# One matmul loop of a fused attention and MLP kernel: 64-column stationary blocks split into 32-column ones, in the first chunk only

## The chip, the cores and the metric

The kernel runs on one core of a Trainium2 chip. The metric is the device time of one execution in microseconds (us); the median of several runs is compared. Five engines work side by side on a core, each through its own list of instructions: TensorE (PE, the matrix multiplier; its loads of stationary operands are listed apart as PEld), VectorE (DVE), ScalarE (ACT), GpSimd (POOL) and SyncE (SP, which here issues nearly all DMAs). An instruction waits for others through semaphores.

In a matmul one operand, the stationary one, is loaded into TensorE's 128 by 128 array; the other, the moving one, streams through. The contraction runs over the partitions (rows), and the columns of the stationary operand become the partitions of the output in PSUM. If the stationary operand has fewer rows or columns, the array can be cut into tiles: a form such as 128*64 in the profile means 128 rows by 64 columns, so that two such tiles lie side by side in the array. Which of them is used follows from the output's partitions.

## The reference, cut to what matters

Inputs are fp32: q, k, v and alpha of (B=4, H=8, S=768, D=48), and an MLP from 384 to 1536 and back.

```python
for t in range(S):
    state = alpha[:, :, t, :, None] * state + np.einsum('bhd,bhe->bhde', k[:, :, t], v[:, :, t])
    y[:, :, t] = np.einsum('bhd,bhde->bhe', q[:, :, t], state)
...
x = y.transpose(0, 2, 1, 3).reshape(B, S, H * D)
xn = (x - mu) / np.sqrt(var + 1e-06) * g_ln
out = x + np.maximum(xn @ w_ch1, 0.0) @ w_ch2
```

The recurrence is computed in chunks. Within a chunk, y is the masked matrix of scores (q scaled by the running product of alpha, k by its inverse) times v, plus q times the state that the chunk began with.

## The kernel before, in words

The sequence is cut into six chunks of 128 positions, and the work into 24 blocks (chunk c, batch b). One block's attention is the generator `attention(c, b)`. The eight heads are counted as `i` (0 or 1) and `p` (0 to NP - 1 = 3). HS = 64 is half a chunk, and `halves[s]` the partitions of half `s`.

A block goes through: Ln of alpha on ScalarE (L342); its running sum by a triangular matmul (L347 in chunk 0, L354 later); two Exp on ScalarE (L357, L358); k and q scaled on VectorE (L360, L362); both turned by TensorE (L414) and copied out as kT and qT (L418); scores on TensorE (L427 in chunk 0, L442 later); masked copies into the tile `at` on VectorE (L451 in chunk 0, L456 later); the state's update on TensorE (L471), on VectorE and, after chunk 0, GpSimd; then y on TensorE, copied with its sum by ScalarE (L519), the layer norm, and the turned x for the MLP (L565, L567).

Chunk 0 (`whole` in the code) differs: there is no earlier state, so y is the product of `at` and v alone, over all 128 positions at once. The tile `at` is (128, NP, 2, 2, 64): key positions on partitions, then p, i, the half s of the queries, and 64 queries. L497 takes a stationary block of 128 by 64, streams the 48 columns of one head's v through it, and writes 64 partitions of the bank `yps0`. So a block of chunk 0 has 4 x 2 x 2 = 16 such matmuls, and there are four blocks. Chunks 1 to 5 use the other branch (L507), with half-chunks of 64 rows.

The order in which the generators advance is written out by hand in the string `ORDER`, one letter for one step: a to x are the 24 attention blocks (a to d are chunk 0), Y, Z, P, Q chunk 0's MLP, M, V and others the later MLPs, A to H the rounding of the weights. Every engine executes its instructions in the order that results. All of chunk 0's y is one step of each block.

## Time and profile before

| | |
|---|---|
| median of 3 runs | 419.16 us (416.6 to 420.09) |
| the profiled execution, own time | 417.81 us |
| its span, first to last instruction | 416.0 us |
| granted TensorE clock | 1.00 |
| the costliest two lines, matmuls of the MLP in chunks 1 to 5 | L892 32% and L714 31% of the chain that ended last |
| L497, the changed line | 1% of that chain |
| bytes moved by DMA | 61.26 MB, mean 147 GB/s |

How to read it: the span is one execution recorded by the profiler. Busy time of an engine counts the time in which at least one of its instructions was running; matmuls are pipelined, so that neighbouring ones overlap and a busy TensorE is not one at its peak. An fp32 matmul leaves two load records and two matmul records; a transpose by TensorE leaves one of each. The timeline merges neighbouring instructions of a kind into one row with the start of the first, the length up to the end of the last, and their count; the brackets behind it hold the idle time of the engine just before and what ended it. "issue" is time in which the engine waited for nothing that the profile shows.

### The profile page before, as it was taken

To read this page: it belongs to the slowest core of one execution; us is meant where nothing else is said; L and a number is where in the kernel's file an instruction comes from. 1 tells how busy PE (TensorE), PEld (TensorE's weight loads), DVE (VectorE), ACT (ScalarE), POOL (GpSimd) and SP (SyncE) were. 2 spreads that over 40 slices of the span, in tenths; PEclk is the share of its full clock that TensorE was granted. 3 is DMA by queue.
4 is the path that set the end of the run, shared out by engine and by line. 5 is a ranking of instruction groups with operands and counts; after the bars stand their busy time and mean duration, and the time that the engine had idled before them with its cause. 6 is when DMAs were issued, how large, how long until landed. Compare 5 with 4: busy or idle time off the path is not lost.

```text
span 416.0 us, 11451 instructions
## 1 busy us (share of the span) xinstructions
PE 409.0 (98%) x4616; PEld 354.9 (85%) x4616; DVE 292.8 (70%) x554; ACT 217.0 (52%) x522; POOL 122.0 (29%) x134
## 2 busy tenths in 40 slices
PE   7999999999999999999999999999999999999997
PEld 5877888876568889998889998899998889999996
DVE  3897989999997888687268973579533288125754
ACT  4787568774364576245584335773353643245110
POOL 1011013132011562144480254260236321525300
PEclk9999999999999999999999999999999999999999
DMA  8998968888878676945776868536324200000301
GB/s 263 282 272 270 283 141 282 243 169 246 230 139 229 164 151 129 237 100 140 168 144 153 200 167 213 108 45 129 109 58 120 71 1 2 19 0 25 110 20 58
DMA packets 134445, 61.26 MB, mean 147 GB/s; under 512 B 90956, under 2 KB 131276, under 8 KB 134392
## 3 DMA queue, kind: packets, MB, share of 16 engines
q1 hardware_dynamic: 133848, 60.37, 57.5%
q8 instruction: 36, 0.59, 0.6%
q10 hardware_dynamic: 544, 0.17, 0.2%
q14 instruction: 17, 0.14, 0.1%
HBM read 43.12 MB, written 17.39 MB: 145 GB/s over the span
## 4 chain that ended last, share of the span: by engine, by line
PE 94%; ACT 3%; DMA 1%; DVE 0%; issue 0%; SPq 0%; DVEq 0%
PE hps L892 32%; PE ops L714 31%; PE hps L590 8%; PE ops L602 8%; PE yps L507 5%; PE aps L442 3%; PE ups L471 2%; PE tps L414 2%; PE lps L354 2%; DMA ra<-in_alpha_dram 1%; PE aps L427 1%; PE yps L497 1%; PE xps L565 1%; ACT hT L931 0%; ACT lps L358 0%; ACT qT L418 0%
## 5 line engine op out<-in xcount | busy, mean ns | idle before, releaser
L892 PE MATMUL hps<-sum,w 128*128 128x256 f32 x192 | 46.3, 383 | 0.0
L714 PE MATMUL ops<-w,hT 128*128 128x192 f32 x224 | 40.8, 326 | 0.8 <-ACT hT L931 0.8
L892 PEld LDWEIGHTS hps<-sum,w 128*128 128x128 f32 x192 | 35.7, 190 | 6.3 <-ACT u L904 1.7
L738 ACT COPY u<-ops 128x192 f32<-128x192 f32 x30 | 9.5, 316 | 56.4 <-PE ops L714 56.3
L714 PEld LDWEIGHTS ops<-w,hT 128*128 128x128 f32 x224 | 37.2, 190 | 1.4 <-ACT hT L931 1.1
L734 POOL TENSOR_TENSOR ob<-ob,u 128x192 f32<-128x192 f32 x32 | 20.8, 659 | 56.7 <-ACT u L738 33.2
L486 POOL TENSOR_TENSOR mid<-mid,gate 112x192 f32<-112x192 f32 x20 | 14.0, 701 | 77.9 <-DVE mid L484 21.2
L590 PE MATMUL hps<-xT,w 128*128 128x256 f32 x144 | 33.9, 385 | 0.2 <-ACT few L538 0.2
L904 ACT COPY u<-hps 128x512 f32<-128x512 f32 x32 | 18.7, 585 | 28.0 <-PE hps L892 22.1
L892 PE MATMUL hps<-xT,w 128*128 128x256 f32 x136 | 33.3, 379 | 0.0
L602 PE MATMUL ops<-w,hT 128*128 128x384 f32 x96 | 32.6, 491 | 0.0
L590 PEld LDWEIGHTS hps<-xT,w 128*128 128x128 f32 x144 | 26.2, 190 | 4.2 <-ACT few L538 0.4
L904 ACT COPY hT<-hps 128x512 f32<-128x512 f32 x40 | 23.3, 585 | 12.3 <-PE hps L892 12.1
L892 PEld LDWEIGHTS hps<-xT,w 128*128 128x128 f32 x136 | 25.8, 190 | 3.4
L714 PE MATMUL ops<-ws,sum 128*128 128x192 f32 x160 | 28.6, 327 | 0.0
L602 PEld LDWEIGHTS ops<-w,hT 128*128 128x128 f32 x96 | 17.7, 190 | 11.7 <-issue 0.6
L714 PEld LDWEIGHTS ops<-ws,sum 128*128 128x128 f32 x160 | 26.4, 190 | 0.6 <-ACT few L538 0.6
L728 DVE TENSOR_TENSOR ob<-ops,ob 128x192 f32<-128x192 f32 x40 | 13.1, 350 | 16.9 <-POOL ob L734 9.5
L931 ACT ACTIVATE hT<-hT 128x512 f32<-128x512 f32 x40 | 22.9, 621 | 2.1 <-DVE hT L911 2.1
L714 PE MATMUL ops<-ws,hT 128*128 128x192 f32 x128 | 23.4, 326 | 0.0
L714 PE MATMUL ops<-more,sum 128*128 128x192 f32 x120 | 22.2, 328 | 0.0
L731 DVE TENSOR_TENSOR ob<-ob,ops 128x192 f32<-128x192 f32 x35 | 11.8, 349 | 14.0 <-PE ops L714 13.5
(223 smaller groups left out, 1037.9 us busy)
## 6 DMA issues: line engine op xcount, KB each, us to landing
ws<-in_moe_w_ch_dram SPq DMA_DIRECT2D x8, 1152.0 KB
vn<-in_v_dram SPq DMA_DIRECT2D x12, 384.0 KB
kept<-x SPq DMA_DIRECT2D x24, 192.0 KB
ob<-kept SPq DMA_DIRECT2D x24, 192.0 KB
rows<-rj SPq DMA_DIRECT2D x48, 96.0 KB
out_dram<-ob SPq DMA_DIRECT2D x18, 192.0 KB
xrows<-xt SPq DMA_DIRECT2D x64, 48.0 KB
xT<-xrows SPq DMA_DIRECT2D x16, 192.0 KB
```

The source lines that it names most:

```text
L442: nc.tensor.matmul(pair[o][halves[i if o else 1 - i], p, s], k_of[rs, p, s], q_of[rs, p, s], start=True, stop=True)
L486: nc.gpsimd.tensor_mul(new, new, by)
L507: nc.tensor.matmul(yps[j][halves[s], i, p], of, by, skip_group_check=True, start=not (cross and k), stop=k == 1 or not cross)
L590: nc.tensor.matmul(hps, w1[:, f, j * P:(j + 1) * P], xT_of[0][:, f, bs], start=(f == 0), stop=(f == NF - 1))
L602: nc.tensor.matmul(ops_of[b], hT_of[c][:, j, b], w2[:, j], start=(j == 0), stop=(j == NJ - 1))
L714: nc.tensor.matmul(acc, lhs[:, j], rhs[:, j], start=j == 0 and n not in FOLLOWS, stop=j == NT - 1 and n not in FOLLOWS.values(), skip_grou ...
L728: nc.vector.tensor_add(x, acc, x)
L731: nc.vector.tensor_sub(x, x, acc)
L734: getattr(nc.vector if c + 1 == NCB else nc.gpsimd, f"tensor_{op}")(x, x, y)
L892: nc.tensor.matmul(acc[:, i], w, b, start=n not in JOINS and i == 0, stop=n not in JOINS.values(), skip_group_check=True)
L904: nc.scalar.copy(out=copied[n], in_=acc)
L931: nc.scalar.activation(out=x, in_=x, func=AFT.Relu)
```

## The change: 32 queries to a stationary block

In the `whole` branch, the 64 queries of a half are taken in two parts of 32 (`quarters`), each with a matmul of its own: stationary 128 by 32, the same 48 moving columns, 32 output partitions of the same bank. The four parts of the 128 queries lie on four column tiles of 32. The branch for chunks 1 to 5 is untouched.

```diff
         yps = [ps.tile([P, 2, NP, D], FP32, name=f"yps{r}", tag="bank", bufs=6)
                for r in range(1 if whole else 2)]
+        quarters = [slice(u, u + HS // 2) for u in (0, HS // 2)]
+
+        def part(s, o):
+            return slice(HS * s + o.start, HS * s + o.stop)
+
         for p in range(NP):
             if whole:
                 for i in range(2):
                     for s in range(2):
-                        nc.tensor.matmul(yps[0][halves[s], i, p], at[:, p, i, s], vn[:, i, p],
-                                         start=True, stop=True)
+                        for o in quarters:
+                            nc.tensor.matmul(yps[0][part(s, o), i, p], at[:, p, i, s, o],
+                                             vn[:, i, p], start=True, stop=True)
                 continue
```

## The prediction

> **What bounds the kernel now.** I read the page first: the busy shares and the chain of waits.

> ```profile
> PE 409.0 (98%) x4616; PEld 354.9 (85%) x4616; DVE 292.8 (70%) x554; ACT 217.0 (52%) x522; POOL 122.0 (29%) x134
> ...
> PE 94%; ACT 3%; DMA 1%; DVE 0%; issue 0%; SPq 0%; DVEq 0%
> ```

> TensorE is busy for 98% of the span and makes up 94% of the chain; the granted clock is full in all 40 slices. TensorE time saved anywhere is therefore worth its face value unless another engine holds up the same stage. The changed line is L497, so next I asked for that line alone, then for the windows by stage.

> ```profile
> L497 PEld LDWEIGHTS yps<-vn,at x128: 133/138/139, 15.7 to 30.3; 128*64 128x64 f32 x128
> L497 PE MATMUL yps<-vn,at x128: 221/222/258, 15.7 to 30.4; 128*64 128x48 f32 x128
> ...
>   POOL at L525: 7.5, 1
>   ACT x L519: 0.8, 2
> ```

> ```profile
> 15.00:20.00 5.00, 5.00 (x95) 3.76 (x94) 3.86 (x8) 4.16 (x11) 0.00 (x0) 1.00 0.92 247
> 20.00:24.00 4.00, 4.00 (x96) 3.94 (x91) 4.00 (x9) 3.14 (x11) 0.95 (x1) 1.00 1.05 322
> 24.00:28.00 4.00, 3.61 (x101) 2.65 (x101) 3.93 (x7) 3.51 (x11) 0.00 (x0) 1.00 0.93 282
> 28.00:33.00 5.00, 4.80 (x65) 2.87 (x60) 4.08 (x8) 4.97 (x13) 0.95 (x1) 1.00 0.86 216
> 33.00:60.00 27.00, 26.97 (x412) 22.46 (x414) 23.93 (x40) 17.33 (x45) 3.50 (x5) 1.00 0.85 239
> ```

> The line runs only between 15.7 and 30.5 us, while chunk 0's attention is built up. The loop has 4 p by 2 i by 2 s = 16 matmuls in a block and four blocks: 64, and the line shows 128 records, two for each fp32 matmul. In the windows (columns: length, then busy us and count of PE, PEld, DVE, ACT, POOL, clock, DMA) VectorE is full from 20 to 24 us, ScalarE from 28 to 33, and TensorE has holes of 0.39 and 0.20 us. From 33 us TensorE has next to none, so what reaches that point reaches the end.

> The size is read from the timeline: start, length, engine, line, form, count, and in brackets the idle time before.

> ```profile
> 15.69 1.01 PEld L497 LDWEIGHTS yps<-vn,at 128*64 128x64 f32 x32 [0.17 <-issue]
> 15.69 1.14 PE L497 MATMUL yps<-vn,at 128*64 128x48 f32 x32
> 17.57 0.44 PEld L471 LDWEIGHTS ups<-vn,qk 128*48 128x48 f32 x16 [0.60 <-issue]
> 18.06 0.97 PEld L427 LDWEIGHTS aps<-qT,kT 48*128 48x128 f32 x16
> 25.97 1.02 PEld L442 LDWEIGHTS aps<-qT,kT 48*64 48x64 f32 x64
> 36.85 0.45 PEld L471 LDWEIGHTS ups<-vn,qk 64*48 64x48 f32 x32 [0.33 <-issue]
> ```

> **What a group of tiles costs.** 128*64 means 128 rows by 64 stationary columns. L497's s alternates between two column tiles, so its 32 loads are 16 pairs. The merged row ends one load (138 ns) after the last start: (1.01 - 0.138)/15 = 58 ns a pair. L442 has four tiles of 64 columns, 64 loads in 16 fours: (1.02 - 0.135)/15 = 59 ns a four. L471 with 48 columns takes (0.44 - 0.125)/7 = 45 ns a pair at 17.57 and (0.45 - 0.122)/7 = 47 a four at 36.85. L427 with 128 columns: (0.97 - 0.188)/7 = 112 a pair. So a round costs by its columns, not by its number of tiles: about 5 ns plus 0.84 ns a column.

> **What the change does to it.** Each of the 16 matmuls of a block becomes two, with 32 stationary columns each and the same 48 moving columns. That adds 64 matmuls, 128 load records and 128 matmul records over four blocks; multiplications and rounds stay as they are, 16 rounds a block, now of four records on four tiles instead of two on two. No DMA, wait, buffer or other engine's instruction is added, removed or moved. The PSUM bank and the next reader, L519 on ScalarE, are the same.

> Price of a new round: by the columns of its load alone 5 + 0.84 x 32 = 32 ns; but 48 moving columns must also pass. L471, with 48 stationary and 48 moving, gives 45, and cannot tell which 48 sets it; L354, with 384 moving on 64 stationary, shows that the moving side can set the pace (0.88 us for two rounds). The upper end from these rows is L497's own 58, at which splitting brings nothing. I take 45, the only rows with 48 moving that are not held by 64 loaded columns. A block then takes 16 x 45 = 0.72 us instead of 16 x 58 = 0.93: 0.21 us less. Four blocks: 0.84 us, between 0 (at 58) and 16 x 26 x 4 = 1.66 us (at 32).

> [...]

> **How much of it reaches 33 us.** Block 0, 15.69: L354 follows at 16.76 on TensorE, and its last input, the ScalarE Ln, ended at 16.37, so 0.2 us goes through; VectorE's masked copy at 19.25 had waited 0.97 us on TensorE's scores and moves by the same. Blocks 1 and 2, 20.13 to 22.17: ScalarE's copy of y at 22.21 waited 0.35 for them, and its copies of kT and qT follow, on which TensorE's scores at 24.88 wait 0.39. Here up to 0.6 us can pass. But VectorE works from 19.25 to 29.7 nearly without a gap and only had the first 0.2; block 3 at 29.47 starts on VectorE's release. Behind block 3, ScalarE is 4.97 of 5.00 us busy, so that block's 0.2 is mostly hidden. Between 0.2 and 0.84 of the sum arrive; I take 0.5, since ScalarE, which carries the chain from 27.8 to 32.6, inherits the larger part. If that cover were gone it would be 0.84.

> **The sum.** The profiled execution took 417.81 us: a span of 416.0 and 1.81 around it. It becomes 417.3. The median of the three runs is 1.35 above that execution, and I carry the difference: 419.16 - 0.5 = 418.7.

> **Rivals.**

> 1. *No gain.* The round is set by something that doesn't shrink with the columns, or ScalarE and VectorE swallow all of it: 419.2. For it: the windows from 20 to 33. Against: the copy at 22.21 and the scores at 24.88, which did wait.

> 2. *A pace per record.* No row has four column tiles on the same 128 rows; L442 and L471 have two row halves by two columns. If the rows can feed only two column tiles at a time, 64 records of a block go in 32 pairs: at 45 ns 1.44 us (0.51 more a block, 2.0 in all), at the present 29 ns a record 1.86 (0.93 more, 3.7 in all). That gives 421.2 to 422.9, still within 1%. A fixed toll on every record does the same from L497's own 29 ns. [...] For it: every group with 128 rows in the trace goes in pairs. Against: 11 ns a record in L471 shows that issuing is no limit, and the two column tiles of L497 run side by side.

> 3. *Slower: the four tiles run one after the other.* If a load into a 32-column tile has to wait for the stream of its neighbour, the 64 records take 45 ns each: 2.88 us instead of 0.93, 1.95 more a block, 7.8 in all, at most about 0.8 of it covered in the holes named above: 426.2 to 427.0. It decides over 1% from about (0.93 + 1.05)/64 = 31 ns a record. For it: the form is untried in this trace. Against: with half the column groups the same rows show starts side by side. That the tiles do not run concurrently is also how the change could fail to do what it says.

> 4. *Faster by over 1%* would need 4.2 us, more than the four blocks' 3.7 us; it could come only from a later stage falling into another order, and TensorE has no waits there to give back.

> **How the numbers follow.** Forecast 0.60; rival 1 0.10; rival 2 0.10; rival 3 0.17; rival 4 0.03. One per cent, 4.2 us, is about what a measurement of this kernel can tell from no change: its three runs spread over 3.5. Within 1% lie the forecast, rival 1 and nearly all of rival 2: 0.79. Slower 0.18, faster 0.03. Range: 417.0 (the 1.7 us bound gives 417.5, and 0.5 for the runs' scatter) to 422.9 (the end of rival 2); it leaves out rivals 3 and 4.

> **What would show it.** L497 must show 256 loads of 128*32 and 256 matmuls. The merged load row of block 0 should be about 0.8 us (0.72 less one round, plus one load of some 0.11) instead of 1.01: near 0.6 means the 32 ns price, near 1.0 no gain, near 1.5 or 1.9 rival 2, near 2.9 rival 3. ScalarE's copy at 22.21 should start near 21.6, TensorE's first hidden product, 32.66 now, near 32.2, and the stages after it should keep their lengths. I am wrong if that product moves later, or if TensorE shows new holes after 33 us.

## The result, and the profile after

The changed kernel took 422.59 us (median of 16 runs, 420.69 to 427.38) beside 419.17 for the kernel before (16 runs): a ratio of 1.0081, with a 95% interval from 1.0055 to 1.0106, which leaves out the longest execution. So it became some 3.4 us slower, by less than 1%, where 0.5 us less was forecast. The profiled execution took 420.94 us with a span of 419.1, against 417.81 and 416.0.

The page of the changed kernel: busy times, the queue that carries instructions (packets, MB, share of time), and the chain by engine.

```profile
PE 408.9 (98%) x4744; PEld 353.9 (84%) x4744; DVE 293.0 (70%) x554; ACT 216.8 (52%) x522; POOL 120.1 (29%) x134
...
q8 instruction: 37, 0.61, 0.6%
...
PE 92%; ACT 3%; DMA 2%; issue 1%; SPq 1%; DVE 0%; DVEq 0%
```

The same queue in the page of the kernel before:

```profile
q8 instruction: 36, 0.59, 0.6%
```

TensorE has 128 load records and 128 matmul records more and the same busy time; the other engines execute as many instructions as before. There is one packet of instructions more, and the chain has 1% of "issue". Where, the timeline of the changed kernel shows:

```profile
15.26 0.89 PE L503 MATMUL yps<-vn,at 128*32 128x48 f32 x64
...
19.54 1.62 PE L503 MATMUL yps<-vn,at 128*32 128x48 f32 x126
24.25 0.27 PE L503 MATMUL yps<-vn,at 128*32 128x48 f32 x2 [3.09 <-issue]
24.45 1.52 PE L414 MATMUL tps<-consts,qk 128*112 128x128 f32 x12
...
31.84 0.89 PE L503 MATMUL yps<-vn,at 128*32 128x48 f32 x64
```

```profile
15.26 0.75 PEld L503 LDWEIGHTS yps<-vn,at 128*32 128x32 f32 x64 [0.17 <-issue]
```

The four tiles do run side by side: a block's 64 load records take 0.75 us where 32 took 1.01, and with 110 ns for the last load (0.75 - 0.110)/15 = 43 ns a round of four. From its start to the next line's, block 0's y takes 0.81 us (15.26 to 16.07) where it took 1.07. But at the end of the y of blocks 1 and 2, with 126 of the 128 matmul records done and only the last matmul of block 2 to come, TensorE stands still for 3.09 us, and no wait in the profile accounts for it: that matmul uses the same tiles `at` and `vn` as the records just before it. ScalarE's copy of y waits for it, in the same timeline:

```profile
24.56 0.49 ACT L525 ACTIVATE x<-yps 128x384 f32<-128x384 f32 x1 [3.44 <-PE yps L503]
```

The windows of the changed kernel (length, then busy us and count of PE, PEld, DVE, ACT, POOL, clock, DMA share, GB/s):

```profile
20.00:24.00 4.00, 1.16 (x103) 1.02 (x90) 3.96 (x9) 0.72 (x3) 0.00 (x0) 1.00 1.06 309
...
33.00:60.00 27.00, 26.52 (x406) 21.68 (x405) 23.46 (x40) 18.18 (x48) 4.28 (x6) 1.00 0.80 226
```

A ledger of the two profiled executions, by starts: block 0's y begins 0.43 us earlier in this one (TensorE waited 0.30 us instead of 0.87 for the Ln of alpha at 7 us, before anything that the change touches), saves 0.26; blocks 1 and 2 cost 2.95 more (the stop, less what the 126 records saved); block 3 saves 0.25; the hole ahead of the first hidden product, 0.20, is 0.47 now. That product starts at 35.05 instead of 32.66, 2.39 later, and the span ends 3.1 later. Some 0.6 us of the rest come at 141 us, where the Ln of one block starts late; that was not followed up.

Part of the 3.4 us does not show in this trace, whose granted clock is full to the end of the span. In 12 of the 16 executions the mean granted clock was 0.991 to 0.996 (median 423.02 us without the longest); in the other four it was 1.0 (median 421.6). In the 53 executions of the kernel before that were measured beside the experiments it was never under 0.999. What such a mean consists of is shown with pad16 below.

### The profile page after: what moved, and what is told of

Read it like the earlier page. It is cut to its first block, busy times and chain, and to the rows that moved or that the text cites. A ratio compares the mean times of both kernels' runs of the same rounds, so it can differ in the third digit from the quotient of the medians.

```text
span 419.1 us, 11706 instructions
## 1 busy us (share of the span) xinstructions
PE 408.9 (98%) x4744; PEld 353.9 (84%) x4744; DVE 293.0 (70%) x554; ACT 216.8 (52%) x522; POOL 120.1 (29%) x134
## 4 chain that ended last, share of the span: by engine, by line
PE 92%; ACT 3%; DMA 2%; issue 1%; SPq 1%; DVE 0%; DVEq 0%
PE ops L720 31%; PE hps L898 30%; PE hps L596 8%; PE ops L608 8%; PE yps L513 4%; PE ups L471 2%; PE aps L442 2%; PE tps L414 2%; PE lps L354 2%; DMA ra<-in_alpha_dram 1%; PE aps L427 1%; DMA vn<-in_v_dram 1%; PE yps L503 1%; PE xps L571 1%; ACT la L342 0%
## 5 line engine op out<-in xcount | busy, mean ns | idle before, releaser
L486 POOL TENSOR_TENSOR mid<-mid,gate 112x192 f32<-112x192 f32 x20 | 12.0, 600 | 75.0 <-DVE mid L484 42.2
L608 PE MATMUL ops<-w,hT 128*128 128x384 f32 x96 | 32.6, 491 | 0.0
L486 POOL TENSOR_TENSOR st<-st,gate 112x192 f32<-112x192 f32 x16 | 14.5, 905 | 25.8 <-DVE st L484 25.8
```

The costliest lines, as they stand in the source:

```text
L486: nc.gpsimd.tensor_mul(new, new, by)
L608: nc.tensor.matmul(ops_of[b], hT_of[c][:, j, b], w2[:, j], start=(j == 0), stop=(j == NJ - 1))
```

## The experiments

**Theory F (fetch).** TensorE's instructions arrive in packets of 16 KB (0.61 MB in 37 packets), 256 instructions each (256 more records, one packet more), and TensorE ran out of them. In this trace it had executed 705 recorded instructions when it stopped (692 loads and matmuls, 12 waits for semaphores and a drain); the next packet began to move at 21.89 us, when it already stood still, and landed at 22.84. **Rival T (tiles):** the stop belongs to the new form. A rival without a letter: the last matmul waits for data that the profile doesn't show.

Of the first four runs, one keeps the amount of instructions and changes the form, two keep the form and shift the instructions against the packets, and one moves a large DMA out of the packet's way.

**rows64.** The old 64 columns, split by rows.

```diff
-nc.tensor.matmul(yps[0][halves[s], i, p], at[:, p, i, s], vn[:, i, p], start=True, stop=True)
+for j in range(2):
+    nc.tensor.matmul(yps[j][halves[s], i, p], at[halves[j], p, i, s],
+                     vn[halves[j], i, p], start=True, stop=True)
```

> In the trace of the changed kernel TensorE stood still for 3.09 us before the last matmul of block 2's y, after 705 of its recorded instructions. Theory F (fetch): it had run out of instructions; 256 of them arrive in one 16 KB packet, and the change put 192 more ahead of this point. Rival T (tiles): the stop belongs to the form, four 128-by-32 tiles. Here chunk 0's y is split by rows instead, on four 64-by-64 tiles into two banks, with the same number of instructions as the change; y is taken from the first bank alone, so chunk 0 leaves the later half of the keys out. F: a stop of 2.3 to 3.1 us at the same place (both blocks take some 0.4 us longer, which comes off the stop). T: no stop in this line.

The timeline of this kernel:

```profile
20.33 2.26 PE L498 MATMUL yps<-vn,at 64*64 64x48 f32 x126
25.13 0.31 PE L498 MATMUL yps<-vn,at 64*64 64x48 f32 x2 [2.53 <-issue]
```

The same stop at the same record, 0.56 us shorter, in a kernel that has no 32-column tile (422.5 us, one run, beside 417.71). T falls.

**plus32 and plus64.** The change, with tiny matmuls in the warm-up.

```diff
+for u in range(32):    # 64 in plus64
+    nc.tensor.matmul(idle[32 * (u % 4):32 * (u % 4) + 32, :1], zero[:, :32], zero[:, :1],
+                     start=True, stop=True)
```

> The change, with 32 tiny matmuls (128 instructions, half a packet) added to the warm-up at the start, while TensorE waits for alpha anyway. F: the packet's edge falls 128 instructions earlier in the work, at the end of block 1's y, and the 256 before it then reach back to block 0's y, some 4.2 us of work: the stop shrinks from 3.1 to at most 1 us and moves to that place. T, and any theory of data that block 2 waits for: 3 us before the last matmul of block 2, as in the changed kernel.

> The same with 64 tiny matmuls, 256 instructions, one whole packet. F: the edge falls on the same matmul again, now after some 961 instructions, and the stop is back: 2.5 to 3.5 us before the last matmul of block 2. If the stop came from the number of instructions since the start and not from a period of 256, it would come one packet earlier in the work, before block 1's y, and not here.

The timeline of plus32:

```profile
20.19 0.88 PE L506 MATMUL yps<-vn,at 128*32 128x48 f32 x62
23.08 0.95 PE L506 MATMUL yps<-vn,at 128*32 128x48 f32 x66 [2.02 <-issue]
```

and of plus64:

```profile
23.93 0.25 PE L474 MATMUL ups<-vn,qk 128*48 128x48 f32 x2 [1.52 <-issue]
24.11 1.87 PE L506 MATMUL yps<-vn,at 128*32 128x48 f32 x126
29.40 0.27 PE L506 MATMUL yps<-vn,at 128*32 128x48 f32 x2 [3.43 <-issue]
```

They took 421.6 and 428.74 us beside 417.71. The place obeys F to the record. In plus32 the stop comes half a packet earlier in the work, after 62 of the 128 matmul records; in plus64 it is back before the last two, now after 961 instructions instead of 705, and one packet ahead of it, after 705, there is another. A matmul that waits for data would not move so. The size doesn't fit: plus32 was to lose at most 1 us and lost 2.02, and 1.09 more after instruction 1217. The packet moved no earlier than 20.77 us there, although TensorE had entered the packet before it at 16.53. The time of plus64 holds more than its stops: block 0's y begins 2.80 us later than in the changed kernel (18.06 against 15.26), and for 3.41 us from 29.74 the granted clock is 0.5.

**late_load.** The change, with w1's first piece loaded later (two letters A of the order string moved).

> The change, with the first piece of w1 (1152 KB) loaded later, so that it is not in the DMA queues while the packet of instructions is wanted (the order string has two letters moved; TensorE's instructions stay the same). F: the packet lands earlier after TensorE needs it, and the stop shrinks to 0.5 to 2.3 us. T: 3.1 us, unchanged. The kernel as a whole may be slower, since the rounding of this piece then waits.

A stop of 2.60 us at the same record: shorter by 0.5, where F wanted at most 2.3 us left. With that load out of the way the packet still began at 21.79 us, 2.07 after TensorE had entered the packet before it (2.53 in the changed kernel). So this load is not the main cause of the packet's lateness. The kernel took 426.74 us: TensorE waited 4.43 us for a block's layer norm on VectorE, which had waited for the piece, and from 36.50 to 43.32 us the granted clock was 0.5.

**not2, not0 and only3** leave some blocks in the old form.

```diff
-for o in quarters:
+for o in quarters if b != 2 else [slice(0, HS)]:    # not0: b != 0; only3: b == 3
```

> The change in blocks 0, 1 and 3 only; block 2 of chunk 0 keeps its 64-column blocks. F: 64 instructions fewer stand ahead of the packet's edge, which then falls into the scores of chunk 0's last block (L427) some 3.5 us later, when the packet is there: no stop over 0.5 us in the y, and the three blocks keep their gain of about 0.24 us each, so 0.2 to 0.7 us faster than before: ratio 0.998 to 1.000. T: a stop that goes with the four-tile form stays in blocks 0 or 1, ratio 1.004 to 1.008.

> The change in blocks 1, 2 and 3 only. Blocks 1 and 2, where the stop was, are exactly as in the changed kernel; only 64 instructions fewer stand before them. F: no stop in these two blocks, at most 0.7 us in the scores behind them; ratio 0.997 to 1.002. T: 3.1 us before the last matmul of block 2, ratio 1.006 to 1.010.

> The change in block 3 only, whose y comes after the packet's edge and behind which ScalarE is full. F: no stop, a y 0.24 us shorter, of which little arrives: ratio 0.998 to 1.001. T: a stop of its share, over 0.5 us, in this block.

Measured: not2 1.0011 (0.9991 to 1.0031), not0 1.0039 (1.0015 to 1.0062), only3 1.0067 (1.0038 to 1.0095): all three above F's ranges, not2 by less than its interval. In the y of chunk 0 there is no stop over 0.5 us in any of the three: in not0, blocks 1 and 2 are exactly those of the changed kernel, and 64 instructions fewer ahead of them took the 3.09 us away (0.34 us of idle time are left, in block 3). But only3, which adds the least, is far slower than F allowed, and the stop that T would put into its y is not there. The waits of TensorE in only3 (waited for: us in total, times, longest):

```profile
PE yps L513 <- issue: 1.7, 1, 1.7
PE aps L442 <- DMA kT<-rows: 1.3, 1, 1.3
```

and the first of them in its timeline:

```profile
220.09 0.20 PE L513 MATMUL yps<-mid,qT 48*64 48x48 f32 x1 [1.71 <-issue]
```

This is a line that the change does not touch, 190 us behind the change, after instruction 6081 = 705 + 21 x 256. In not2 and not0 there is one like it after 7617 = 705 + 27 x 256:

```profile
PE ups L471 <- issue: 1.2, 1, 1.2
```

(that is not2's row). Of the changed kernel, whose 256 added instructions are one packet exactly, no such stop is seen behind chunk 0. F explains all three if it is taken further than I had: the added instructions shift every later packet edge too.

**moving24.** The kernel before, each matmul split by its moving columns.

```diff
+for o in (slice(0, D // 2), slice(D // 2, D)):
+    nc.tensor.matmul(yps[0][halves[s], i, p, o], at[:, p, i, s], vn[:, i, p, o], start=True, stop=True)
```

> The kernel before, with the 48 moving columns of chunk 0's y split in two of 24 and the 64 stationary columns kept, on the two old tiles: the same number of instructions as the change, in the old form. F: each block takes 1.87 us instead of 0.94, and at the same place, before the last matmul of block 2, TensorE stops for what is left, 0.5 to 1.8 us. T: blocks of 1.87 us and no stop.

No stop, where F wanted one of 0.5 to 1.8 us: the 422.31 us (one run) come from the longer blocks. T had fallen already; F's size missed again. The 256 instructions of the packet took TensorE 3.70 us here, and the next packet had landed 2.48 us before they were through.

**pad16, pad64 and restored** test F taken further: padding of no use at all, in front of `hidden`'s first matmul, in the old form and in not2.

```diff
+for u in range(16 if h == 0 and j == 0 else 0):    # 64 in pad64; restored: not2 with 16
+    nc.tensor.matmul(hps[32 * (u % 4):32 * (u % 4) + 32, 0, :1], ident[:, :32], ident[:, :1],
+                     start=True, stop=True)
```

> The kernel before, all y in the old form, with 16 tiny matmuls (64 instructions) put ahead of TensorE's first hidden product at 32.66 us: pure padding, whose results are overwritten, some 0.3 us of work in a place where TensorE waits 0.2 us. It moves the packet edges of everything behind by 64 instructions, as the change in block 3 alone did (ratio 1.0067, with a stop of 1.9 us after instruction 6081, at 218 us). F: the same again, at least one stop of 1 to 2 us whose place is 705 plus a multiple of 256, ratio 1.003 to 1.009. Rival P (padding costs its own time only): ratio 1.000 to 1.001, no stop.

> The same with 64 tiny matmuls, 256 instructions, one whole packet: behind it every edge falls on the same work as in the kernel before. They take some 1.0 us. F: no stop over 0.5 us behind 40 us, ratio 1.000 to 1.004, so less than with a quarter of the padding although more is done. P: four times the cost of 16, whatever that is; a stop may come anywhere.

> The change in blocks 0, 1 and 3 (192 instructions; alone it gave a ratio of 1.0011 and one stop of 1.36 us after instruction 7617, at 276 us) and 16 tiny matmuls ahead of the first hidden product, so that 256 are added up to there, one whole packet. F: no stop after instruction 7617 nor any other over 0.5 us; the gain in the y, 3 x 0.24 us, less some 0.3 for the padding: ratio 0.996 to 1.000. P: 1.001 to 1.002, with the stop at 276 us as it was.

Measured: pad16 1.0059 (1.0030 to 1.0089), pad64 1.0019 (0.9996 to 1.0043), restored 0.9988 (0.9972 to 1.0004). The padding of pad16 and of pad64, in their timelines, and the stop of pad16:

```profile
32.03 0.43 PE L590 MATMUL hps<-consts 128*32 128x1 f32 x32
...
217.09 0.20 PE L507 MATMUL yps<-mid,qT 48*64 48x48 f32 x1 [1.92 <-issue]
```

```profile
31.73 1.25 PE L590 MATMUL hps<-consts 128*32 128x1 f32 x128
```

Sixteen matmuls of 0.43 us in all made the kernel some 2.5 us slower, with a stop at the edge where only3 had its own; sixty-four, of 1.25 us, brought no stop, and their ratio asks for no more than their own time.

The stop is not all that pad16 pays for. Behind it the granted clock (the 1.00, 0.50 and 1.00 in these windows) is halved for 3.41 us, and eight matmul records of L717 take 2.65 us where the same eight in only3 take 1.46:

```profile
217.10:218.60 1.50, 1.50 (x19) 0.88 (x19) 0.94 (x2) 0.46 (x2) 1.31 (x1) 1.00 0.38 20
218.60:222.00 3.40, 3.40 (x12) 3.14 (x11) 0.00 (x0) 2.15 (x8) 0.00 (x0) 0.50 0.54 152
222.00:225.00 3.00, 3.00 (x34) 2.77 (x36) 1.74 (x5) 0.09 (x1) 0.00 (x0) 1.00 0.52 149
```

```profile
219.62 2.65 PE L717 MATMUL ops<-w,hT 128*128 128x192 f32 x8
```

By an estimate from these rows, half of 3.41, the stretch can lose up to 1.7 us. Five of pad16's eight executions have a mean clock of 0.995 or 0.996 and a median of 421.55 us, the other three 0.999 or 1.0 and 419.51, 1.1 above the kernel before. The same stretch of 3.41 us stands in the traces of not0 (from 278.96 us, behind its stop), rows64 (26.33) and only3 (140.10, behind the 1.3 us wait for kT and not behind its stop), and in none of the executions of pad64 and restored is the mean under 0.999. So the ratios measure a stop or another wait of TensorE and, in some executions, a slower stretch after it. Whether a wait brings the clock down was not tested: behind the 3.09 us of the changed kernel's trace it stayed at 1.00.

In restored the stop after 7617 is gone; the list of its TensorE's waits has no row of "issue" at all:

```profile
PE lps L287 <- DVE more L284: 1.1, 1, 1.1
PE ops L723 <- ACT hT L940: 0.8, 1, 0.8
PE aps L427 <- ACT qT L418: 0.6, 2, 0.4
PE tps L414 <- DVE qk L360: 0.4, 1, 0.4
PE aps L442 <- DMA kT<-rows: 0.2, 1, 0.2
```

So P (padding costs its own time only) falls, and F holds in all three. restored is the change in three of four blocks, with padding up to a whole packet; it took 417.78 us beside 418.44, but its interval still touches 1.

The stops at packet edges, worked out from the starts in the traces (the stop is taken between two starts, and so some 0.2 us longer than the idle time in the timeline, in which the last record still runs):

```
kernel     edge  work of the packet  stop   next packet lands  TensorE goes on
                 before it, us       us     us                 after landing, us
after       705        1.60          3.29        22.84              1.41
rows64      705        2.22          2.75        23.68              1.44
late_load   705        1.54          2.80        22.72              1.33
plus32      705        4.33          2.22        21.71              1.38
plus32     1217        3.81          1.30        31.69              1.63
plus64      705        4.69          1.73        22.54              1.39
plus64      961        1.84          3.63        27.98              1.41
not0        705        4.51          0.23        23.51              1.48
not0        961        4.47          0.55        28.74              1.28
not0       7617        1.96          1.63       277.15              1.42
not2       7617        1.94          1.36       276.20              1.39
only3      6081        1.76          1.93       218.66              1.43
pad16      6081        1.76          2.13       215.57              1.52

none of these: shortest packet of the kernel
before     7361        3.31
moving24   7617        3.31
pad64      7617        3.52
restored   7617        3.31
```

Every edge is 705 plus a multiple of 256, and TensorE goes on 1.28 to 1.63 us after the missing packet has landed, each time. Three smaller gaps of the kind, 0.25 to 0.30 us between starts and 1.33 to 1.57 us behind a landing, stand at 1217 in the kernel before and in pad16 and at 1473 in rows64. The four kernels at the end have no packet of less than 3.31 us of work. But the work of a packet does not decide alone: four packets of 2.37 to 2.69 us in plus32, only3 and pad16 passed without a stop. There the next packet had begun to move 0.7 to 1.6 us before TensorE entered them; at the 13 stops it began 0.85 to 4.24 us after.

## Why the prediction was wrong, point by point

- **A round of four tiles at 45 ns:** right, 43 ns; that the loaded columns set a round, bounded by the 48 that move, fits it (58 ns with 64 loaded columns, 45 in L471 with 48 loaded and 48 moving) but was not shown by itself, and 0.81 us for block 0 against 1.07 is the gain that was priced at 0.21.
- **"No DMA, wait, buffer or other engine's instruction is added, removed or moved":** this is the step that failed. The instructions are themselves brought by DMA: one packet came on top, 37 for 36, and 192 of the records lie ahead of the edge after 705, so that this edge moved back from the scores that follow (26.79 us in the kernel before, with the packet landed 2.69 us earlier) into the densest stretch of the program: 256 instructions in 1.60 us. "11 ns a record in L471 shows that issuing is no limit" was read from 32 records; a packet is 256. The sum has no term for the stop, 3.09 us, nor for a clock under 1.0, which the profile before gave no reason for and most executions of the changed kernel have.
- **Rivals 2 and 3** priced a loss, up to 3.7 and up to 7.8 us, by mechanisms that did not occur: nothing ran two by two or one after the other. A fixed toll on every record, at L497's own 29 ns, would have made 116 ns of four records; they took 43. That the time came out where rival 2 has it, and so inside the range of 417.0 to 422.9, is chance.
- **"Between 0.2 and 0.84 of the sum arrive":** too hopeful, also without the stop. From the start of block 0's y to the first hidden product the kernel before takes 16.97 us (15.69 to 32.66); not2, with three blocks in the new form and no stop, takes 17.11 (15.31 to 32.42), and there TensorE waits 0.52 us for VectorE's rounding of the weights (L264). That is half of rival 1: in these traces VectorE, which I had seen to be full from 19 us on, swallows the gain. In restored it is 17.04 us (14.89 to 31.93), with the padding standing in the same hole. A delay does arrive: the changed kernel takes 19.79 us.
- **"What reaches that point reaches the end":** right in the main, 2.39 us there and 3.1 at the end.

Not settled: what decides when a packet starts to move. In the runs that stopped after 705 it began between 20.77 and 22.58 us, while TensorE entered the packet before it anywhere from 16.53 to 20.25; moving one large load out of the way changed little. So F gives the places exactly, and the sizes only roughly. The DMA engines are full there (a share of 1.05 from 19.3 to 24.3 us in the changed kernel), but around the stop of not2 at 276 us the share is 0.19, and the packet still comes too late: full queues are not needed for a stop. The wait for kT, 1.3 us at 139 us in only3 and 1.1 us in not0, was not followed up either.

## What to carry to other kernels

Count an engine's instructions before splitting small matmuls: in this kernel each fp32 matmul is four, and wherever 256 of them, from one packet edge to the next, were through in under 2.3 us, TensorE stopped for 1.4 to 3.6 us with "issue" as the only sign (stops of 0.2 to 2.2 us came in packets of 3.8 to 4.7 us, too). A change of the count shifts all later edges, so a slower kernel may have paid far from the edit (only3 paid 190 us behind it); look for the new "issue" rows, and try the same edit padded to a multiple of 256 before judging it. A tuned kernel may owe part of its time to where its edges happen to fall, as this one did: sixteen useless matmuls cost it 0.6%, by a stop and, in five of eight executions, a lower granted clock.

## What the runs showed of the hardware that was not expected

Four column tiles of 32 on the same 128 rows do work side by side in fp32: starts 7 ns apart, 43 ns for four with 48 moving columns, against 58 for two of 64.

Behind some waits of TensorE stands a stretch at a granted clock of 0.5: 3.41 us in five traces of these kernels (rows64, plus64, not0, only3, pad16), 6.83 in late_load. The mean clock was under 0.997 in 12 of 16 executions of the changed kernel, 5 of 10 of only3, 5 of 8 of pad16, 2 of 10 of not0 and 1 of 12 of not2, and in none of the 77 of pad64, restored and the kernel before beside the experiments.
